# A routed expert layer on one core: the residual split of the second weight half moves from GpSimd to VectorE in the tail slots

## The chip, the cores and the metric

One core of one Trainium2 chip. The time is the device time of one execution in microseconds (us). Three runs of the kernel before gave 1162.65, 1166.04 and 1166.87 us; their median is 1166.04 us.

## The reference

A causal convolution of 7 taps with softmax weights (8 heads, 24 channels each) runs over 8 sequences of 2880 rows and 192 channels. Its 23040 rows go to 16 experts: the row's best of 4 groups, then the best of 4 experts in that group. Cut to what matters here:

```python
for g in range(G):
    mask_g = g_idx == g
    xg = x[mask_g]
    ... # e_idx, e_w from softmax(xg @ w_expert[g])
    for e in range(Eg):
        mask_e = e_idx == e
        h = np.maximum(xg[mask_e] @ w1[g, e], 0.0)   # 192 -> 1024
        ye = h @ w2[g, e]                            # 1024 -> 192
        out[tok_idx] = g_w[...] * e_w[...] * ye      # rows of that expert
```

All of it is float32, and the results have to be of float32 quality.

## The kernel before, in words

**Routing, then slots.** The convolution and the routing run unit by unit and write each row and its id to tables in memory. The expert layer works in slots. A big slot takes 256 rows of one expert (two tiles of 128), a small one 128 rows. For each slot GpSimd issues indirect DMAs that gather the rows (tile `xg`, line 648) and, at its end, others that scatter the results to `out` (line 750).

**Split operands.** Each float32 operand is split in two parts that TensorE takes: a high part, written by ScalarE, and the residual, written as a subtraction. A weight set has four splits in `split(k)`: k = 0 makes `ah` (ScalarE, line 613) and `al` (line 614) out of the first 128 rows of w1; k = 1 makes `bh` (ScalarE, line 621) and `bl` (line 622) out of the other 64 rows, which are loaded twice; k = 2 and 3 make the halves of `cw` (lines 628 and 629) out of w2. The dictionary `eng` says which engine makes a residual; without an entry it is VectorE. The loads land in six `raw` buffers, four for each set, so a split that ends sets a buffer free for a load of a later set, which SyncE's queue issues.

**A big slot** has four steps. In each, `hidden` does 20 matmuls (line 679), ScalarE makes `hh` (line 684) and VectorE `hl` (line 685); three steps later `back` does 16 matmuls (lines 697 and 701) into two banks `po`. `finish` scales both banks on ScalarE (line 748), adds two halves on VectorE (`ys`, line 749) and scatters. **A small slot** has two steps: `hidden_small` (line 714), a transposition (line 722), `hh` on ScalarE (line 725) and `hl` on VectorE (line 726), and `back_small` with four matmuls on `hh` (line 734) and four on `hl` (line 740).

**The plan.** The first 62 of 98 slots are big ones. Then come nine groups: a small tail slot, two big slots of one regular expert, and a big tail slot. Tail slots take the rows left over of an expert that a table names at run time. In a group there are thus three weight sets: small tail, regular, big tail.

**The order of the work.** The slot loop calls `split_one` at given steps, but in each engine's queue the instructions stand in the order in which the framework's planner lists them by its own estimates of cost, dependences and places in the text; what is ready early can be listed ahead of its slot. Once listed, an engine takes them strictly in that order. So an instruction that waits holds up all that stand behind it in its queue.

The place that matters is in `open_slot`, where a tail slot's weights are opened and its first argument pair, row offsets, is read at run time:

```python
if pi == "tail":
    W = weights(*tail_regs(lambda c: tab[0][0:1, e, c:c + 1], 2), {1: nc.gpsimd})
```

Of the kernel before, what the change touches and what calls it, by code (L numbers as in the profile page):

```python
# [35 lines left out]
def conv_moe_kernel(  # L36
# [10 lines left out]
    nc = tc.nc  # L47
# [9 lines left out]
    def pin(on, ins):  # L57

        return tc.keep_in_program_order(ins) if on and pinned[0] else ins
# [529 lines left out]
    def weights(r1, r2, eng=None):  # L589
        eng = eng or {}  # L590
        raw = [wraw.tile([P, F], F32, name="raw") for _ in range(4)]
        ra, rb = raw[0], raw[1]
        HF = NF // 2
        rc = [r[:, 0:HF * D].rearrange("p (f d) -> p f d", d=D) for r in raw[2:]]
        npin[0] += 1
        hold = tc.keep_in_program_order if NPIN[0] < npin[0] <= NPIN[1] else lambda ins: ins
        hold(nc.sync.dma_start(out=ra, in_=w1f[bass.ds(r1, P), :]))
        hold(nc.sync.dma_start(out=rb[0:D2], in_=w1f[bass.ds(r1 + P, D2), :]))
        hold(nc.sync.dma_start(out=rb[D2:P], in_=w1f[bass.ds(r1 + P, D2), :]))
        for k in range(2):  # L600
            hold(nc.sync.dma_start(
                out=rc[k], in_=w2f[bass.ds(r2 + k * HF * P, HF * P), :].rearrange("(f p) d -> p f d", p=P),
            ))
        W = {}

        def split(k):
            if k == 0:
                W["ah"] = ah = wsp.tile([P, F], F32R, name="ah")
                W["al"] = al = wsp.tile([P, F], F32R, name="al")
                if 8 in eng:  # L610
                    nc.gpsimd.tensor_copy(out=ah, in_=ra)
                else:
                    pin(PINA, nc.scalar.activation(out=ah, in_=ra, func=AF.Copy))  # L613
                eng.get(k, nc.vector).tensor_tensor(out=al, in0=ra, in1=ah.bitcast(F32), op=ALU.subtract)  # L614
            elif k == 1:
                W["bh"] = bh = wsp.tile([P, F], F32R, name="bh")
                W["bl"] = bl = wsp.tile([P, F], F32R, name="bl")
                if 9 in eng:
                    nc.gpsimd.tensor_copy(out=bh, in_=rb)
                else:  # L620
                    pin(PINB, nc.scalar.activation(out=bh, in_=rb, func=AF.Copy))  # L621
                eng.get(k, nc.vector).tensor_tensor(out=bl, in0=rb, in1=bh.bitcast(F32), op=ALU.subtract)
            else:
                if k == 2:
                    W["cw"] = wsp.tile([P, NF, 2, D], F32R, name="cw")
                cw = W["cw"]
                fs = slice((k - 2) * HF, (k - 1) * HF)
                pin(PINW, nc.scalar.activation(out=cw[:, fs, 0, :], in_=rc[k - 2], func=AF.Copy))  # L628
                eng.get(k, nc.vector).tensor_tensor(  # L629
                    out=cw[:, fs, 1, :], in0=rc[k - 2], in1=cw[:, fs, 0, :].bitcast(F32), op=ALU.subtract,  # L630
                )

        W["todo"] = [lambda k=k: split(k) for k in range(4)]
        return W
# [9 lines left out]
    def gather(ids, known, n=2):  # L644
        xs = xg[nslot[0] % NXG]
        nslot[0] += 1
        for t in range(n):
            nc.gpsimd.indirect_dma_start(  # L648
                out=xs[:, t, :], out_offset=None, in_=xcd[0:known, :],
                in_offset=bass.IndirectOffsetOnAxis(ap=ids[:, t:t + 1].bitcast(U32), axis=0),  # L650
                bounds_check=known - 1, oob_is_err=False,
            )
        return xs
# [251 lines left out]
    def stages_to(n):  # L905
        extra = sum(max(0, stages(n) - i * SKEW2) for i in range(1, LIVE2)) if n < NU else 0
        return sum(stages(u) for u in range(n)) + extra
# [7 lines left out]
    def step():  # L915

        if routed[0] < NU and len(live) < lead[1] and (not live or max(live, key=lambda a: a[0])[1] >= (lead[0] or SK[min(routed[0], len(SK)) - 1])):
            u = routed[0]
            live.append([u, 0, unit(u, xin0 if u == 0 else None)])
            routed[0] += 1  # L920
        if not live:
            return
        done[0] += 1
        cur = live.pop(0)
        cur[1] += 1
        try:
            next(cur[2])
            live.append(cur)
        except StopIteration:
            pass  # L930
# [17 lines left out]
    tab = [None]  # L948
# [19 lines left out]
    def open_portion(pi):  # L968
        need, spe = portions[pi]
        rows = spe * 2  # L970
        idp = const.tile([P, E, rows], I32, name=f"idp{pi}")
        if pi == 0:
            pin(PINI, IQ.dma_start(
                out=idp,
                in_=idtab[0:E * CAP].rearrange("(e r) c -> e r c", e=E)[:, 0:P * rows, :].rearrange(
                    "e (p r) c -> p e (r c)", r=rows),
            ))
        else:
            ci = const.tile([1, E], I32, name=f"ci{pi}")
            nc.vector.tensor_copy(out=ci, in_=cons[0:1])  # L980
            _, base = nc.values_load_multi_w_load_instructions(
                ci, engines=[ET.SP], min_val=0, max_val=DUMMY - P * rows, skip_runtime_bounds_check_because=OOB_WHY,
            )
            for e in range(E):
                nc.sync.dma_start(
                    out=idp[:, e],
                    in_=idtab[bass.ds(base[e], P * rows), :].rearrange("(p r) c -> p (r c)", r=rows),
                )
        idps[pi] = idp
        consume(spe * SLOT)  # L990
        if pi + 1 == len(portions):
            late.append(open_tail())

    def tail_regs(get, n):
        return [
            nc.values_load(
                get(c), engines=[ET.SP], min_val=0, max_val=mv, skip_runtime_bounds_check_because=OOB_WHY,
            )
            for c, mv in ((0, (E - 1) * D), (1, (E - 1) * F), (2, DUMMY))[:n]
        ]  # L1000
# [18 lines left out]
    def tiles(i):  # L1019

        return 1 if plan[i][0] == "tail" and plan[i][1] >= NBIG else 2

    def open_slot(i):
        if i >= len(plan):
            return
        pi, e, s = plan[i]
        if closing:
            wait[0] -= 1
            if wait[0] <= 0 or closing[0] == pi:
                open_portion(closing.pop())  # L1030
        while pi != "tail" and pi not in idps:
            step()
            if closing:
                open_portion(closing.pop())
        rate[0] = max(
            [(stages_to(portions[q][0]) - done[0]) / (max(starts[q] - MARGIN - i, 1) * 2 * NF)
             for q in starts if q not in idps] + [0.0])
        if late:
            next(late[0], None)
        if pi == "tail":  # L1040
            W = weights(*tail_regs(lambda c: tab[0][0:1, e, c:c + 1], 2), {1: nc.gpsimd})
            ids = idps["tail"][:, e]
            known = N
        else:
            W = pre.pop(e if pi == 0 else None, None) or weights(e * D, e * F, PENG(pi, e)) if s == 0 else opened[i - 1][0]
            ids = idps[pi][:, e, 2 * s:2 * s + 2]
            known = sum(n for _, n in units[:portions[pi][0]]) * BT
        opened[i] = (W, ids)
        gathered[i] = gather(ids, known, tiles(i))
# [3 lines left out]
    while routed[1] < portions[0][0]:  # L1053
# [3 lines left out]
        for i in [i for i, kk in enumerate(KPRE) if kk == k]:  # L1057
            e, q = divmod(i, 5)
            if q == 0 and e < 2:
                pre[e] = weights(e * D, e * F, {k: nc.gpsimd for k in PREG[e]})  # L1060
            elif e < 2 and 4 * e + q <= KN:
                split_one(pre[e])
        k += 1
    open_slot(0)
    open_slot(1)
    for e in range(2, 2 + PRE2):
        pre[e] = weights(e * D, e * F)
# [78 lines left out]
    for i, (pi, e, s) in enumerate(plan):  # L1146
# [3 lines left out]
        W, ids = opened[i]  # L1150
# [10 lines left out]
        for f2 in range(steps):  # L1161
# [25 lines left out]
            if f2 == 0:  # L1187
                open_slot(i + 2)
# [39 lines left out]
```

## Time and profile before

| what | before |
|---|---|
| median of three runs | 1166.04 us (1162.65 to 1166.87) |
| the profiled execution | 1165.88 us, of it span 1164.1 us |
| PE (TensorE matmul) busy in the span | 1111.3 us, 95% |
| PEld (TensorE weight load) | 1079.1 us, 93% |
| DVE (VectorE) | 802.9 us, 69% |
| ACT (ScalarE) | 690.9 us, 59% |
| POOL (GpSimd) | 495.4 us, 43% |
| mean granted TensorE clock | 0.985 |

A row of a timeline is: start in us from the span's start, length in us, engine, line, operation, tile written and tiles read, partitions x elements, count, and in brackets how long the engine sat idle just before and what ended that. A row of the waits is: who waited, for whom, us in total, times, longest. TensorE's matmuls overlap, so two of its rows can cover the same time. SP is SyncE; a q behind an engine's name is its sequencer.

### The profile page before, as it was taken

The page shows a single profiled execution, that of the slowest core. Times are in us where ns is not written, and L with a number is a line of the kernel's source. Part 1 is how long each engine was busy: PE and PEld are TensorE (multiplying, and loading weights), DVE is VectorE, ACT ScalarE, POOL GpSimd, SP SyncE. Part 2 cuts the span into 40 slices and gives each one's busy share as a digit, 9 for nine tenths or more (in the row PEclk, how much of TensorE's full clock was granted, in tenths as well). Part 3 has the DMA queues.
Part 4 walks back from the last instruction along what each step waited for, and adds up shares of the span by engine and source line. Part 5 has one row for each costly group of instructions (what it writes and reads, how often), then busy time and mean ns, then how long its engine had stood idle before and what let it go on. Part 6 is the DMA issues. An engine that isn't in the chain of part 4 may idle for free. (4 is left out here: it accounts for less than half of the span.)

```text
span 1164.1 us, 23639 instructions
## 1 busy us (share of the span) xinstructions
PE 1111.3 (95%) x8468; PEld 1079.1 (93%) x8468; DVE 802.9 (69%) x1667; ACT 690.9 (59%) x1326; POOL 495.4 (43%) x432
## 2 busy tenths in 40 slices
PE   6889899999999999999999999999999999999995
PEld 5768899999999999999999999999999999999995
DVE  3666987887877676575678666666766777767672
ACT  4535556657665565646655555555676666767662
POOL 1003423333435343434435444445455655646542
PEclk9978999999999999999999999999999999999999
DMA  8989879988994565536454656545666577676740
GB/s 181 236 201 223 187 183 225 215 227 222 233 249 132 139 176 131 138 104 158 121 151 88 170 93 175 149 123 142 175 164 195 165 200 208 172 188 172 194 114 21
DMA packets 194090, 196.17 MB, mean 169 GB/s; under 512 B 49443, under 2 KB 171181, under 8 KB 193966
## 3 DMA queue, kind: packets, MB, share of 16 engines
q1 hardware_dynamic: 127424, 140.43, 45.9%
q0 software_dynamic: 18528, 36.09, 12.2%
q10 hardware_dynamic: 48014, 18.10, 7.7%
q8 instruction: 67, 1.10, 0.4%
q14 instruction: 57, 0.47, 0.1%
HBM read 159.08 MB, written 36.85 MB: 168 GB/s over the span
## 5 line engine op out<-in xcount | busy, mean ns | idle before, releaser
L697 PE MATMUL po<-cw,hh 128*128 128x384 f32 x1424 | 443.4, 369 | 1.4 <-ACT ys L748 1.4
L679 PE MATMUL ph<-xa,ah 128*128 128x256 f32 x1424 | 389.9, 296 | 3.6 <-DVE hl L685 2.0
L701 PE MATMUL po<-cw,hl 128*128 128x192 f32 x1424 | 356.8, 251 | 0.0
L648 POOL DMA_INDIRECT xg<-xcd,idp x160 | 181.3, 1133 | 377.7 <-ACT ys L748 338.0
L685 DVE SCALAR_TENSOR_TENSOR hl<-ph,hh 128x512 fp32r<-128x512 f32 x356 | 242.8, 686 | 142.5 <-ACT hh L684 127.9
L684 ACT ACTIVATE hh<-ph 128x512 fp32r<-128x512 f32 x356 | 211.3, 596 | 214.6 <-PE ph L679 166.6
L679 PEld LDWEIGHTS ph<-xa,ah 128*128 128x128 f32 x1424 | 271.5, 191 | 6.7 <-DVE hl L685 2.8
L701 PEld LDWEIGHTS po<-cw,hl 128*128 128x128 f32 x1424 | 272.8, 192 | 1.9
L697 PEld LDWEIGHTS po<-cw,hh 128*128 128x128 f32 x1424 | 268.8, 189 | 4.6 <-ACT ys L748 2.3
L750 POOL DMA_INDIRECT out<-ys,idp x160 | 191.9, 1199 | 75.3 <-issue 48.9
L679 PE MATMUL ph<-xb,bh 128*128 128x256 f32 x712 | 201.9, 284 | 0.1
L679 PE MATMUL ph<-xb,bl 128*128 128x256 f32 x712 | 201.8, 284 | 0.0
L679 PE MATMUL ph<-xa,al 128*128 128x256 f32 x712 | 201.6, 283 | 0.0
L748 ACT ACTIVATE ys<-po,xg 128x384 f32<-128x384 f32 x187 | 105.7, 580 | 94.2 <-PE po L701 66.8
L749 DVE TENSOR_TENSOR ys<-ys 128x192 f32<-128x192 f32 x187 | 82.3, 447 | 90.9 <-ACT ys L748 84.7
L679 PEld LDWEIGHTS ph<-xa,al 128*128 128x128 f32 x712 | 136.9, 192 | 1.8
L679 PEld LDWEIGHTS ph<-xb,bl 128*128 128x128 f32 x712 | 136.7, 192 | 0.0
L679 PEld LDWEIGHTS ph<-xb,bh 128*128 128x128 f32 x712 | 135.9, 191 | 0.8 <-issue 0.5
L629 DVE TENSOR_TENSOR cw<-raw,cw 128x768 fp32r<-128x768 f32 x132 | 125.2, 951 | 11.4 <-ACT cw L628 5.3
L628 ACT ACTIVATE cw<-raw 128x768 fp32r<-128x768 f32 x132 | 110.7, 843 | 0.1
L614 DVE TENSOR_TENSOR al<-raw,ah 128x1024 fp32r<-128x1024 f32 x66 | 80.8, 1224 | 38.3 <-ACT ah L613 27.2
L613 ACT ACTIVATE ah<-raw 128x1024 fp32r<-128x1024 f32 x66 | 70.1, 1062 | 32.7 <-PE ph L679 13.8
(222 smaller groups left out, 1444.5 us busy)
## 6 DMA issues: line engine op xcount, KB each, us to landing
raw<-in_moe_w SPq DMA_DIRECT2D x132, 384.0 KB
raw<-in_moe_w SPq DMA_DIRECT2D x66, 512.0 KB
raw<-in_moe_w SPq DMA_DIRECT2D x132, 256.0 KB
xcd<-xc ACTq DMA_DIRECT2D x13, 742.5 KB
xin<-in_x SPq DMA_DIRECT2D x7, 1134.0 KB
xin<-in_x SPq DMA_DIRECT2D x6, 1039.5 KB
xcd<-xcb ACTq DMA_DIRECT2D x13, 360.0 KB
xg<-xcd,idp POOLq DMA_INDIRECT x160
```

The source lines that it names most:

```text
L614: eng.get(k, nc.vector).tensor_tensor(out=al, in0=ra, in1=ah.bitcast(F32), op=ALU.subtract)
L628: pin(PINW, nc.scalar.activation(out=cw[:, fs, 0, :], in_=rc[k - 2], func=AF.Copy))
L629: eng.get(k, nc.vector).tensor_tensor(out=cw[:, fs, 1, :], in0=rc[k - 2], in1=cw[:, fs, 0, :].bitcast(F32), op=ALU.subtract,)
L648: nc.gpsimd.indirect_dma_start(out=xs[:, t, :], out_offset=None, in_=xcd[0:known, :], in_offset=bass.IndirectOffsetOnAxis(ap=ids[:, t:t + ...
L679: nc.tensor.matmul(out=hp[:, j], lhsT=wgt[:, fs], rhs=xx, start=i == 0, stop=i == len(ops) - 1)
L684: nc.scalar.activation(out=hh, in_=hp, func=AF.Relu)
L685: nc.vector.scalar_tensor_tensor(out=hl, in0=hp, scalar=0.0, in1=hh.bitcast(F32), op0=ALU.max, op1=ALU.subtract,)
L697: nc.tensor.matmul(out=oo[t][:, 0:2 * D], lhsT=hh[:, j, ts], rhs=cw[:, f].rearrange("p a d -> p (a d)"), start=f == 0, stop=False,)
L701: nc.tensor.matmul(out=oo[t][:, 0:D], lhsT=hl[:, j, ts], rhs=cw[:, f, 0, :], start=False, stop=f == NF - 1,)
L748: nc.scalar.activation(out=ys[:, t, :], in_=oo[t][:, 0:2 * D], func=AF.Copy, scale=g)
L749: nc.vector.tensor_tensor(out=ys[:, t, 0:D], in0=ys[:, t, 0:D], in1=ys[:, t, D:2 * D], op=ALU.add)
L750: nc.gpsimd.indirect_dma_start(out=outviews[nscat[0] % len(outviews)], out_offset=bass.IndirectOffsetOnAxis(ap=ids[:, t:t + 1].bitcast(U32 ...
```

## The change

The tail slots' call loses its dictionary, so their 18 residuals `bl` are made by VectorE's `tensor_tensor` instead of GpSimd's. Operands, shapes and places in the text stay as they are. Nothing else is edited; the planner lists all queues anew.

```diff
         if pi == "tail":
-            W = weights(*tail_regs(lambda c: tab[0][0:1, e, c:c + 1], 2), {1: nc.gpsimd})
+            W = weights(*tail_regs(lambda c: tab[0][0:1, e, c:c + 1], 2))
             ids = idps["tail"][:, e]
```

The line in `split` that it decides:

```python
eng.get(k, nc.vector).tensor_tensor(out=bl, in0=rb, in1=bh.bitcast(F32), op=ALU.subtract)
```

## Rows read from the trace of the kernel before

**Rows 1.** Busy us of each engine in stretches, then granted clock, DMA share, GB/s.

```profile
450.00:790.00 340.00, 337.81 (x2643) 334.97 (x2643) 229.18 (x464) 193.27 (x358) 148.48 (x132) 1.00 0.54 134
821.60:1121.20 299.60, 292.31 (x2180) 284.75 (x2179) 212.56 (x319) 200.81 (x354) 164.53 (x130) 1.00 0.68 185
```

**Rows 2.** Waits of all engines, stretch 790 to 1164.

```profile
ACT bh L621 <- DMA raw<-in_moe_w: 14.8, 7, 2.7
...
PEld po L740 <- DVE hl L726: 10.0, 8, 1.6
...
PE po L740 <- DVE hl L726: 7.4, 7, 1.3
```

**Rows 3.** Timeline of PE at the small slots' second steps.

```profile
871.60 0.69 PE L740 MATMUL po<-cw,hl 128*128 128x192 f32 x4 [1.03 <-DVE hl L726]
...
943.97 0.69 PE L740 MATMUL po<-cw,hl 128*128 128x192 f32 x4 [0.71 <-DVE hl L726]
...
980.24 0.69 PE L740 MATMUL po<-cw,hl 128*128 128x192 f32 x4 [0.95 <-DVE hl L726]
...
1016.27 0.69 PE L740 MATMUL po<-cw,hl 128*128 128x192 f32 x4 [0.75 <-DVE hl L726]
...
1126.31 0.69 PE L740 MATMUL po<-cw,hl 128*128 128x192 f32 x4 [1.31 <-DVE hl L726]
...
1128.06 0.34 PE L697 MATMUL po<-cw,hh 128*128 128x384 f32 x1
```

**Rows 4.** Timeline of DVE around the last small slot.

```profile
1113.91 1.22 DVE L622 TENSOR_TENSOR bl<-raw,bh 128x1024 fp32r<-128x1024 f32 x1
1115.05 0.42 DVE L666 TENSOR_TENSOR xa<-pm,xa 128x256 fp32r<-128x256 f32 x1
...
1121.67 2.51 DVE L749 TENSOR_TENSOR ys<-ys 128x192 f32<-128x192 f32 x2 [3.28 <-ACT ys L748]
1124.11 0.95 DVE L629 TENSOR_TENSOR cw<-raw,cw 128x768 fp32r<-128x768 f32 x1
1124.98 0.68 DVE L685 SCALAR_TENSOR_TENSOR hl<-ph,hh 128x512 fp32r<-128x512 f32 x1
1125.58 0.68 DVE L726 TENSOR_TENSOR hl<-pm,hh 128x512 fp32r<-128x512 f32 x1
```

**Rows 5.** Line 749 over the span: duration ns min/median/max, first and last start.

```profile
L749 DVE TENSOR_TENSOR ys<-ys x187: 294/358/2201, 124.6 to 1154.6; 128x192 f32<-128x192 f32 x187
```

**Rows 6.** Groups by line, stretch 821 to 1130: count, busy us, mean ns, idle before.

```profile
L749 DVE TENSOR_TENSOR ys<-ys 128x192 f32<-128x192 f32 x59 | 37.2, 645 | 35.3 <-ACT ys L748 35.0 <-issue 0.2
```

**Rows 7.** Line 622 over the span, by engine: duration ns min/median/max, first and last start.

```profile
L622 DVE TENSOR_TENSOR bl<-raw,bh x48: 1154/1217/1227, 54.4 to 1113.9; 128x1024 fp32r<-128x1024 f32 x48
...
L622 POOL TENSOR_TENSOR bl<-raw,bh x18: 2384/2398/2407, 803.8 to 1121.3; 128x1024 fp32r<-128x1024 f32 x18
```

**Rows 8.** Timeline of POOL, the last group's two residuals.

```profile
1104.33 2.40 POOL L622 TENSOR_TENSOR bl<-raw,bh 128x1024 fp32r<-128x1024 f32 x1
...
1121.26 2.39 POOL L622 TENSOR_TENSOR bl<-raw,bh 128x1024 fp32r<-128x1024 f32 x1 [6.38 <-ACT bh L621]
```

**Rows 9.** Timeline of ACT around the last small slot.

```profile
1120.12 1.06 ACT L621 ACTIVATE bh<-raw 128x1024 fp32r<-128x1024 f32 x1 [2.61 <-SPq L1091]
1121.08 1.03 ACT L748 ACTIVATE ys<-po,xg 128x384 f32<-128x384 f32 x2
1122.01 0.84 ACT L628 ACTIVATE cw<-raw 128x768 fp32r<-128x768 f32 x1
1122.74 0.59 ACT L684 ACTIVATE hh<-ph 128x512 fp32r<-128x512 f32 x1
1123.22 0.60 ACT L725 ACTIVATE hh<-pm 128x512 fp32r<-128x512 f32 x1
...
1127.04 0.58 ACT L748 ACTIVATE ys<-po,xg 128x384 f32<-128x384 f32 x1 [1.02 <-PE po L740]
```

**Rows 10.** Timeline of DVE beside the small set's residual, last group.

```profile
1105.68 0.69 DVE L685 SCALAR_TENSOR_TENSOR hl<-ph,hh 128x512 fp32r<-128x512 f32 x1 [1.65 <-ACT hh L684]
1106.65 0.69 DVE L685 SCALAR_TENSOR_TENSOR hl<-ph,hh 128x512 fp32r<-128x512 f32 x1 [0.27 <-ACT hh L684]
```

## The prediction

> **What bounds the kernel now.** I read the busy shares first: TensorE is near full, so only what keeps it waiting can move the time. The stretches come next [rows 1]. In the 340 us of regular slots TensorE is busy 337.81 us, 2.2 us short; in the tail groups 292.31 of 299.60, 7.3 us short, at the full granted clock of 1.00 in both. VectorE is busy 212.56 of 299.60 there (71%), GpSimd 164.53 (55%). The waits of that part say who holds TensorE up: nearly all of it is one line, the four small-slot matmuls on `hl`, which wait for VectorE's line 726, 7.4 us in 7 cases; its weight loads wait 10.0 us in 8 cases for the same [rows 2]. The two views tell of the same gaps and differ because matmuls overlap, so the true loss lies between 7.4 and 10.0 us; I take the middle, 8.7. The PE timeline shows the cases: 1.03, 0.71, 0.95, 0.75 us, and 1.31 in each of the last three groups, of which one stands there [rows 3]. Nothing in that list names the GpSimd residual itself.
>
> **Why VectorE is late there.** In the last group it runs the pair of `ys` additions in 2.51 us, then a `cw` half, an `hl`, and at 1125.58 the `hl` that TensorE waits for [rows 4]. An addition of this shape has a median of 358 ns over the span, but a longest one of 2201 [rows 5]; the 59 of the tail have a mean of 645 [rows 6], which is 59 x (645 - 358) = 16.9 us too much, 1.88 us for each of nine groups. The first of the pair starts at 1121.67, while GpSimd works on its residual from 1121.26 to 1123.65 [rows 8], and VectorE goes on only after that: 2.51 us from 1121.67 end at 1124.18. So the residual on GpSimd, 2398 ns [rows 7], costs VectorE 2.51 - 2 x 0.36 = 1.79 us in the very stretch that TensorE waits on. This is the residual of the big tail slot's set, which the planner lists two slots ahead, in the small slot. The other nine (the small set's) lie beside `hl` instructions with an input in PSUM, which take their usual 0.69 us [rows 8, 10] and are not held up.
>
> **Removed.** 18 GpSimd instructions of 2398 ns, 43.2 us of an engine that is idle 45% of the stretch and for which TensorE is not seen to wait there: worth nothing by itself. With them goes GpSimd's wait for `bh`, 6.38 us ahead of the last one [rows 8], behind which gathers and scatters stood; these are issued earlier, and I count nothing for it. With them goes also the stall of 1.79 us in nine groups.
>
> **Added.** 18 VectorE instructions of 1217 ns [rows 7], 1.14 us from start to next start (1113.91 to 1115.05) [rows 4], together 20.5 us. Nothing in the trace shows them in their new places. The ends are 0, all in idle time, and +20.5 us, all on TensorE's path. For the nine of the small sets I take 0: `bl` would follow its `bh`, where GpSimd started at 1104.33, and VectorE sits idle 1.65 us before 1105.68 and 0.27 before 1106.65 [rows 8, 10], which is more than 1.14. With that cover gone it is 1.14 us late for one `hl`, 10.3 us in nine groups at most, and only where TensorE waits for that `hl`, which the waits do not show.
>
> For the nine of the big sets the place decides. When `bh` is done, VectorE has been idle for a while (3.28 us before the pair [rows 4]) and nothing else is ready, so I expect the planner to list `bl` there, ahead of the `ys` pair. It then starts about when GpSimd's did, 1121.26, and the rest follows: 1.14 for `bl`, 2 x 0.36 for the pair, 0.87 and 0.60 from start to start for `cw` and `hl` [rows 4]. Line 726 starts at 1121.26 + 1.14 + 0.72 + 0.87 + 0.60 = 1124.59, 0.99 us earlier than 1125.58. ScalarE's inputs are there in time: `ys` by 1122.11, `cw` by 1122.85, `hh` by 1123.33 and 1123.82 [rows 9]. The new wait, VectorE on `bh`, has the pair, `cw`, `hl` and line 726 behind it, and TensorE behind these; but their inputs stand behind `bh` in ScalarE's queue as well [rows 9], so they would wait anyway.
>
> **Buffers and queues.** `bl` is done earlier (1.22 us after `bh` instead of 2.40), so the `raw` buffer that it frees goes to SyncE's next load sooner, never later. ScalarE's `bh` waits for such a load 7 times, 14.8 us [rows 2]; I leave that as it is. No DMA is added.
>
> **Sum.** The waits of TensorE shrink by 0.99 each: 1.03 to 0.04, the three of 1.31 to 0.32, the others to nothing, so about 1.0 us stays. 8.7 - 1.0 = 7.7 us off. The profiled execution took 1165.88 us (span 1164.1, and 1.8 around it), which makes 1158.2; the median of the runs is 0.16 above it, so 1158.4. What is late next in those places is `hh` of line 725, done at 1123.82 [rows 9].
>
> [...] The additions are float32 with two inputs in SBUF, and the long one that is shown ends when GpSimd's residual does [rows 4, 8]. [...]
>
> **Rivals.**
> 1. *Half the gain.* `bl` is listed behind the `ys` pair instead of ahead of it. Then line 726 starts at 1121.67 + 0.72 + 1.14 + 0.87 + 0.60 = 1125.00, 0.58 earlier; 7 x 0.58 = 4.1 us by TensorE's waits, up to 4.8 at the scale of 8.7: 1161.6 us. For it: the pair comes from an older slot and may be preferred. Against it: idle time ahead of it.
> 2. *The wait moves.* The planner does not seem to know the stall (it listed the pair there), so in its reckoning line 726 comes later than before, and it may list the ten matmuls of the next `hidden` half (1.2 us) ahead of the four on `hl`. The small slot's bank is then emptied 1.2 us later, and the next `back` waits for it: today line 748 ends at 1127.62 and `back` starts at 1128.06, 0.44 us of room [rows 3, 9]. So 1.2 - 0.44 = 0.76 us, nine times, 6.8 of the 7.7 us are given back: 1165.3 us, no change.
> 3. *Slower: the stall isn't GpSimd's.* The long `ys` stays at 2.2 us for another reason, for instance its input. Then the pair starts 1121.26 + 1.14 - 1121.67 = 0.73 us later than now and all behind it too: 9 x 0.73 = 6.6 us more, 1172.6 us. It decides from the point where the longest line 749 is still near 2201 ns without GpSimd's residual. Against it: in the row pair GpSimd's end and VectorE's go together, and the excess comes to nine times the stall, as often as GpSimd makes such a residual there.
> 4. *More.* `bl` goes behind line 726, in a later gap; the whole wait of 7.4 to 10.0 us goes: 1156 to 1158.6. This counts to the forecast, since the time is nearly the same.
>
> **How the numbers follow.** Forecast with rival 4: 0.60, its own range 1156 to 1160.5. Rival 1: 0.18. Rival 2: 0.13. Rival 3, with any other loss on VectorE's longer queue: 0.09. Faster or slower begins at 0.5%, 5.8 us, about what a measurement of this kernel can tell from no change, so at 1160.2 and 1171.9. Faster: all of the forecast, 0.60. Same: rivals 1 and 2 and a little of rival 3, 0.32. Slower: 0.08. The range begins at the end of the unknown, 10.0 us off and a little for the spread of runs, 1155, and reaches over rivals 1 and 2 to 1167; rival 3 is left out.
>
> **What would show it.** In the changed trace line 749 has no instruction over 0.5 us; 66 residuals of line 622 stand on DVE; in the nine small slots `bl` stands right ahead of the `ys` pair; TensorE's waits for line 726 fall from 7.4 us to about 1; its busy share in the groups rises towards that of the regular slots. The prediction is wrong if those waits go and the time stays (rival 2: look for new waits of line 697 on line 748), or if the long `ys` stays.

## The result, and the profile after

The changed kernel took 1155.69 us (median of 4 runs, 1152.3 to 1159.08) beside 1166.45 us of the kernel before: a ratio of 0.9898, interval 0.9864 to 0.9932. It is faster, as forecast, but by 1.02% where 0.65% stood in the prediction, and 0.9898 lies just below the range's lower end (1155 / 1166.04 = 0.9905). The miss is narrow: the recorded ratio is not the quotient of the two medians, which would be 0.9908, just inside. Timed again, in 12 runs beside 35 of the kernel before, the ratio was 0.9927 (0.9902 to 0.9951), which is 8.5 us of 1161.78. The ratios, here and below, leave out a run more than 1.5% above the fastest of its kernel, one of those 35 and one of the kernel with one input from PSUM.

The profiled execution took 1159.08 us, of it span 1157.3 us. The first and last starts on TensorE of lines 714 and 740 bound the tail stretch, from the first small slot to the last matmul on `hl`; columns are count, ns min/median/max, first and last start in us.

```profile
L714 PE MATMUL ph<-ah,xa x36: 393/404/414, 824.5 to 1109.8; 128*128 128x512 f32 x36
...
L740 PE MATMUL po<-cw,hl x72: 250/274/358, 835.1 to 1119.9; 128*128 128x192 f32 x72
```

It lasts 1119.9 - 824.5 = 295.4 us. In the profile of before the same two starts are 821.7 and 1126.7, 305.0 us apart:

```profile
L714 PE MATMUL ph<-ah,xa x36: 393/404/414, 821.7 to 1115.0; 128*128 128x512 f32 x36
...
L740 PE MATMUL po<-cw,hl x72: 250/274/358, 832.3 to 1126.7; 128*128 128x192 f32 x72
```

So the tail is 9.6 us shorter. The head, in which both kernels have the same instructions in the same order but for the first moved residual, is 2.8 us longer, which is inside its spread between executions (816.2 to 824.5 us in the ten profiles). The busy us of the engines in stretches answer to [rows 1]:

```profile
450.00:790.00 340.00, 339.37 (x2669) 336.45 (x2669) 227.89 (x462) 192.78 (x355) 148.07 (x132) 1.00 0.54 135
824.50:1114.60 290.10, 289.81 (x2168) 283.05 (x2167) 216.05 (x335) 200.16 (x353) 130.47 (x114) 1.00 0.72 191
```

TensorE, the first number behind the length, is now 0.3 us short of full in the tail groups instead of 7.3, while VectorE (third) works more, 216.05 of 290.10 (74%). Both stretches are at the full granted clock (1.00). The waits that answer to [rows 2]:

```profile
DVE bl L622 <- ACT bh L621: 20.7, 8, 2.9
...
ACT bh L621 <- DMA raw<-in_moe_w: 16.8, 7, 2.7
...
PEld po L740 <- DVE hl L726: 1.9, 5, 0.4
```

The matmul row for line 726 (7.4 us in 7 cases) is gone and its weight loads' row fell from 10.0 to 1.9. The new wait is there, VectorE for `bh`, 20.7 us in 8 cases; no wait of TensorE for those instructions follows from it. VectorE, then ScalarE and TensorE around the last small slot, for [rows 4, 9, 3]:

```profile
1115.58 1.23 DVE L622 TENSOR_TENSOR bl<-raw,bh 128x1024 fp32r<-128x1024 f32 x1 [2.39 <-ACT bh L621]
1116.72 0.62 DVE L749 TENSOR_TENSOR ys<-ys 128x192 f32<-128x192 f32 x2
1117.26 0.95 DVE L629 TENSOR_TENSOR cw<-raw,cw 128x768 fp32r<-128x768 f32 x1
1118.13 0.68 DVE L685 SCALAR_TENSOR_TENSOR hl<-ph,hh 128x512 fp32r<-128x512 f32 x1
1118.73 0.68 DVE L726 TENSOR_TENSOR hl<-pm,hh 128x512 fp32r<-128x512 f32 x1
```

```profile
1114.49 1.06 ACT L621 ACTIVATE bh<-raw 128x1024 fp32r<-128x1024 f32 x1 [2.17 <-SPq L1091]
1115.46 1.03 ACT L748 ACTIVATE ys<-po,xg 128x384 f32<-128x384 f32 x2
...
1117.59 0.61 ACT L725 ACTIVATE hh<-pm 128x512 fp32r<-128x512 f32 x1
```

```profile
1118.86 0.86 PE L734 MATMUL po<-cw,hh 128*128 128x384 f32 x4
1119.56 0.60 PE L740 MATMUL po<-cw,hl 128*128 128x192 f32 x4
```

`bl` stands in VectorE's queue right ahead of the `ys` pair, and the pair takes 0.62 us instead of 2.51. From the start of `bh` to that of line 726 there are 4.24 us; before it was 1125.58 - 1120.12 = 5.46. So line 726 is 1.22 us earlier, and line 740 starts with no idle time ahead of it. Lines 749 and 622 over the span, for [rows 5, 7]:

```profile
L749 DVE TENSOR_TENSOR ys<-ys x187: 294/358/423, 125.1 to 1147.8; 128x192 f32<-128x192 f32 x187
```

```profile
L622 DVE TENSOR_TENSOR bl<-raw,bh x66: 1157/1216/1229, 52.9 to 1115.6; 128x1024 fp32r<-128x1024 f32 x66
```

No addition is over 0.5 us, and all 66 residuals are VectorE's. In the queues nothing else moved: TensorE (8468 matmuls), ScalarE (1326 instructions) and SyncE (435 transfers issued) have the same order of instructions in both kernels, VectorE has 18 more, and GpSimd 18 fewer, with its gathers and scatters in the same order.

### The profile page after: what moved, and what is told of

It is laid out like the page before. It is cut to its first block, busy times and chain, and to the rows that moved or that the text cites. A ratio compares the mean times of both kernels' runs of the same rounds, so it can differ in the third digit from the quotient of the medians.

```text
span 1157.3 us, 23621 instructions
## 1 busy us (share of the span) xinstructions
PE 1110.4 (96%) x8468; PEld 1079.6 (93%) x8468; DVE 806.5 (70%) x1685; ACT 691.5 (60%) x1326; POOL 457.2 (40%) x414
## 4 chain that ended last, share of the span: by engine, by line
PE 66%; issue 13%; DVE 7%; DMA 6%; POOL 5%; ACT 2%; POOLq 0%; another core or an unknown queue 0%; SPq 0%; ACTq 0%; DVEq 0%
PE ph L679 26%; PE po L697 16%; PE po L701 8%; PE pm L416 3%; POOL xg L648 3%; DMA raw<-in_moe_w 2%; POOL out L750 2%; PE pm L464 2%; DMA out<-ys,idpt 2%; PE pm L661 1%; PE pm L662 1%; PE pm L434 1%; PE pm L459 1%; DMA idtab<-lsi,rowi 1%; DVE hl L685 1%
## 5 line engine op out<-in xcount | busy, mean ns | idle before, releaser
L749 DVE TENSOR_TENSOR ys<-ys 128x192 f32<-128x192 f32 x187 | 65.4, 356 | 68.9 <-ACT ys L748 59.1
L622 DVE TENSOR_TENSOR bl<-raw,bh 128x1024 fp32r<-128x1024 f32 x66 | 80.3, 1217 | 22.3 <-ACT bh L621 22.0
```

## The experiments

The theory, called "port" (only a name: the runs show which instructions are held up, and for how long, not by what part of the chip): what costs is GpSimd reading SBUF while VectorE wants to read two inputs there, in the nine small slots. Rivals: GpSimd's queue (gathers and scatters held back by the residual's wait), VectorE's load, and something outside the tail. In all kernels below TensorE, ScalarE and SyncE have the order of before, so their traces can be laid side by side. GpSimd's gathers and scatters have it too, except in the kernel with one input from PSUM and the two in which GpSimd works beside VectorE, where some of them change places. The table gives the ratio to the kernel before with its interval, the tail stretch as above, TensorE's matmul waits for line 726, and the longest two-input `ys` addition.

| kernel | runs | ratio | tail, us | waits, us (times) | longest `ys`, ns |
|---|---|---|---|---|---|
| before | 4 | | 305.0 | 7.4 (7) | 2201 |
| before, again | 12 | 0.9999 (0.9974 to 1.0024) | 303.0 | 7.3 (8) | 2198 |
| after | 4 | 0.9898 (0.9864 to 0.9932) | 295.4 | 0 | 423 |
| after, again | 12 | 0.9927 (0.9902 to 0.9951) | 294.6 | 0 | 423 |
| big sets only | 12 | 0.9937 (0.9910 to 0.9964) | 294.3 | 0 | 424 |
| small sets only | 12 | 1.0041 (1.0017 to 1.0065) | 301.3 | 5.6 (7) | 2257 |
| small sets only, again | 12 | 1.0001 (0.9977 to 1.0024) | 303.9 | 8.2 (8) | 2252 |
| one input from PSUM | 12 | 0.9951 (0.9925 to 0.9976) | 294.4 | 0 | 2197 (once, in a slot ahead of the edit) |
| GpSimd reads beside | 6 | 1.0085 (1.0058 to 1.0113) | 309.7 | 10.5 (8) | 2062 |
| GpSimd writes beside | 12 | 0.9933 (0.9903 to 0.9962) | 295.1 | 0 | 425 |

**The changed kernel again**, no edit.

> The changed kernel unedited, timed in more rounds, since four runs leave the gain anywhere between 7.9 and 15.9 us. Theory 'port' (a GpSimd residual that reads SBUF holds up VectorE's ys addition in the nine small slots): the stretch from the first small slot to the last matmul on hl is again near 295.4 us (before: 305.1), and what is beyond 9.7 us in the timed gain is spread between runs, so the ratio settles near 0.992 (1156.5 us beside 1166). Rival 'more': something else in the kernel gained too; then the ratio stays at 0.990 or below and the head up to the first small slot is shorter than 821.7 us as well.

The tail is 294.6 us and the ratio 0.9927. It was not the changed kernel whose first four runs came out low (median 1155.69 us, and 1152.66 now) but the kernel before whose four came out high (1166.45 us, and 1161.78 now). The ratio is not 0.990 or below, and the head lasted 824.4 us here against 821.7 in the profile of before, so nothing points to a gain there; the rival falls.

**Big sets only.**

```diff
-            W = weights(*tail_regs(...), {1: nc.gpsimd})
+            W = weights(*tail_regs(...), {1: nc.gpsimd} if e >= NBIG else None)
```

> Only the nine big tail sets' residual bl goes to VectorE, the nine small sets' stay on GpSimd. Theory 'port': all of the gain, tail stretch 295.4 us, no ys addition over 0.5 us, time as the changed kernel (about 1156). Rival 'queue' (what gains is that GpSimd's queue no longer waits for bh, so gathers and scatters go out earlier): about half the gain, tail stretch near 300 us, time near 1161.

All of the gain with half of the change. The nine small sets' residuals stay on GpSimd, and that costs nothing.

**Small sets only**, the other half, and the same kernel once more.

```diff
-            W = weights(*tail_regs(...), {1: nc.gpsimd})
+            W = weights(*tail_regs(...), {1: nc.gpsimd} if e < NBIG else None)
```

> Only the nine small tail sets' residual bl goes to VectorE, the nine big sets' stay on GpSimd. Theory 'port': no gain, nine ys additions of 2.2 us stay, TensorE waits 7.4 us for line 726, tail stretch 305 us, time about 1166. Rival 'queue': half the gain, tail stretch near 300 us, time near 1161. Rival 'VectorE load' (each residual on VectorE costs TensorE something that the removed stall outweighed): slower than before, by up to 9 x 1.14 = 10 us.

> The small sets' nine residuals on VectorE once more, since 12 runs gave 0.41% slower [0.17, 0.65] where no change was expected, and its profile showed no longer wait. Theory 'port' with spread: the interval takes in 1.000 or misses it by less than 0.2%. Rival 'VectorE load': slower by 0.3 to 0.5% again, with a wait of TensorE for line 685 or for line 726 in the profile that the kernel before does not have.

No gain: the long additions and the waits stay. The first timing said 0.41% slower, the second 0.01%. TensorE's waits for line 726 are 5.6 and 8.2 us, on either side of the 7.4 and 7.3 of before, so I take the first timing as spread; a cost of VectorE's load isn't shown. VectorE and GpSimd in the last small slot of the second profile:

```profile
1115.03 2.58 DVE L749 TENSOR_TENSOR ys<-ys 128x192 f32<-128x192 f32 x2 [2.65 <-ACT ys L748]
...
1119.00 0.68 DVE L726 TENSOR_TENSOR hl<-pm,hh 128x512 fp32r<-128x512 f32 x1
```

```profile
1114.66 2.39 POOL L622 TENSOR_TENSOR bl<-raw,bh 128x1024 fp32r<-128x1024 f32 x1 [5.80 <-ACT bh L621]
```

The pair is held up to 1117.61 while GpSimd reads until 1117.05, as in [rows 4, 8]. That only the other half gains is what "port" says, but it doesn't yet rule out the queue: nearly all of GpSimd's wait for `bh` (53.0 us here, 53.1 in the kernel before) belongs to the big sets. The last pair of kernels does.

**One input from PSUM.** All residuals stay on GpSimd; in the tail the addition takes one half from the bank and scales it itself.

```diff
-            nc.vector.tensor_tensor(out=ys[:, t, 0:D], in0=ys[:, t, 0:D], in1=ys[:, t, D:2 * D], op=ALU.add)
+            nc.vector.scalar_tensor_tensor(out=ys[:, t, 0:D], in0=oo[t][:, D:2 * D], scalar=g,
+                in1=ys[:, t, 0:D], op0=ALU.mult, op1=ALU.add)   # from the tail on; as before ahead of it
```

> All 18 residuals stay on GpSimd as before; in the tail the ys addition reads one half straight from PSUM and scales it itself, so it has one input in SBUF instead of two. Theory 'port': GpSimd no longer holds it up, the additions take about 0.4 us, line 726 starts some 1.7 us earlier, TensorE's waits for it go, tail stretch near 296 us, time near 1157 without any residual moved. Rival 'queue' and any theory by which the residual itself must leave GpSimd: 1166, tail stretch 305 us, and a long addition stays.

The edit begins behind the pair of the first small slot, which keeps its long addition; in the other eight there is none, without moving any residual. The last small slot, VectorE and GpSimd:

```profile
1112.59 0.89 DVE L749 SCALAR_TENSOR_TENSOR ys<-po,xg,ys 128x192 f32<-128x192 f32 x2 [1.60 <-ACT ys L748]
1113.80 1.58 DVE L629 TENSOR_TENSOR cw<-raw,cw 128x768 fp32r<-128x768 f32 x1 [0.32 <-ACT cw L628]
1115.30 0.68 DVE L685 SCALAR_TENSOR_TENSOR hl<-ph,hh 128x512 fp32r<-128x512 f32 x1
1115.90 0.67 DVE L726 TENSOR_TENSOR hl<-pm,hh 128x512 fp32r<-128x512 f32 x1
```

```profile
1112.17 2.38 POOL L622 TENSOR_TENSOR bl<-raw,bh 128x1024 fp32r<-128x1024 f32 x1 [4.66 <-ACT bh L621]
```

The pair with one SBUF input runs inside GpSimd's time at its usual 0.42 us each. The next instruction with two, `cw`, starts at 1113.80 while GpSimd reads until 1114.55, and takes 1.58 us instead of 0.95: here it is the number of SBUF inputs that decides, not the line. Nor is it the operation: line 666, a `tensor_tensor` with one input in PSUM, starts beside the small sets' residuals eight times here and takes its usual 0.28 us.

The time is a different matter. TensorE's waits for line 726 are gone and the tail is 294.4 us, but only part of that comes from the addition. From the start of `bh` to that of line 726 there are 4.88 us instead of 5.47 (medians), so line 726 is 0.59 us earlier and not 1.7, because the stall has moved to `cw`. Reckoned as in the prediction, 0.59 us takes at most 7 x 0.59 = 4.1 us off the 7.4. The rest came in ahead of `bh`. ScalarE's wait for the load of `bh`, 14.8 us before, is short here:

```profile
ACT bh L621 <- DMA raw<-in_moe_w: 2.4, 3, 1.0
```

In every other kernel of the table it is between 13.1 and 16.8 us. GpSimd's gathers and scatters changed places around that load; whether this is why it lands earlier was not tested. So this kernel shows which instruction is held up, and it leaves open how much of its gain is owed to GpSimd's queue.

**GpSimd reads, or only writes, beside the pair.** Two kernels on top of the changed one. Behind `bl` of the big sets, GpSimd works on the raw buffer, which nobody reads any more.

```diff
+                if 99 in eng:  # a mark that the big tail sets carry; the first kernel
+                    nc.gpsimd.tensor_tensor(out=rb, in0=rb, in1=rb, op=ALU.subtract)
+                if 99 in eng:  # the second kernel
+                    nc.gpsimd.memset(rb, 0.0); nc.gpsimd.memset(rb, 0.0)
```

> The changed kernel, and in each of the nine big sets GpSimd does one more tensor_tensor of 128x1024 float32 on the raw buffer behind bl, in place, with a result that nobody reads: it reads SBUF and runs beside VectorE's ys pair and cw half. Theory 'port': a two-input instruction of VectorE that starts meanwhile (the second ys or the cw half) is held up until it ends, so nine instructions of over 2 us come back; line 726 then starts about 5.3 us after bh instead of the 4.3 of before, TensorE waits for it 9 x 2.4 = 22 us against 8.8, tail stretch near 315 us, time 8 to 12 us above the kernel before. Rival (the removed residual was only late work of its own, GpSimd holds nobody up): as the changed kernel, tail stretch 295 us.

> The same place and the same buffer, but GpSimd writes it twice with a memset (about 1 us each, by 0.43 us for 392 columns), so it reads nothing. Theory 'port, reads only' (what is shared is the way in which GpSimd reads SBUF and VectorE reads its second input): no long instruction on VectorE, tail stretch 295 us, time as the changed kernel. Rival 'port, any access' or 'any GpSimd work': VectorE is held up by about 2 us in nine places as beside the reading instruction, tail stretch over 305 us.

VectorE in the first, then in the second, with GpSimd of each behind it:

```profile
1127.00 1.23 DVE L622 TENSOR_TENSOR bl<-raw,bh 128x1024 fp32r<-128x1024 f32 x1 [2.21 <-ACT bh L621]
1128.14 2.33 DVE L749 TENSOR_TENSOR ys<-ys 128x192 f32<-128x192 f32 x2
...
1131.93 0.68 DVE L726 TENSOR_TENSOR hl<-pm,hh 128x512 fp32r<-128x512 f32 x1
```

```profile
1128.37 1.89 POOL L622 TENSOR_TENSOR raw<-raw 128x1024 f32<-128x1024 f32 x1 [7.07 <-DVE bl L622]
```

```profile
1110.90 1.23 DVE L622 TENSOR_TENSOR bl<-raw,bh 128x1024 fp32r<-128x1024 f32 x1 [2.47 <-ACT bh L621]
1112.04 0.62 DVE L749 TENSOR_TENSOR ys<-ys 128x192 f32<-128x192 f32 x2
1112.58 0.96 DVE L629 TENSOR_TENSOR cw<-raw,cw 128x768 fp32r<-128x768 f32 x1
```

```profile
1112.19 0.96 POOL L622 MEMSET raw<- 128x1024 f32 x1 [7.26 <-DVE bl L622]
```

A reading instruction brings the stall back (2.33 us for the pair) and the kernel is 0.85% slower than before; a writing one in the same place, beside the same pair, does nothing to VectorE, whose pair takes 0.62 us. (Of its two memsets one stands beside the pair, 0.96 us; the planner listed the other later. The two kernels have their gathers and scatters in the same order.)

The writing kernel also settles the rival "queue". GpSimd's queue waits there about as long as before (54.9 us for `bl`; before, 53.1 for `bh`), and the first gather behind that wait goes out 1114.72 - 1109.81 = 4.91 us after the start of `bh`, later than the 1123.80 - 1120.12 = 3.68 of before. GpSimd of before, then ScalarE, GpSimd and GpSimd's wait in the writing kernel:

```profile
1123.80 1.05 POOL L648 DMA_INDIRECT xg<-xcd,idpt  x1
```

```profile
1109.81 1.06 ACT L621 ACTIVATE bh<-raw 128x1024 fp32r<-128x1024 f32 x1 [2.26 <-SPq L1091]
```

```profile
1114.72 1.05 POOL L648 DMA_INDIRECT xg<-xcd,idpt  x1 [0.30 <-issue]
```

```profile
POOL raw L622 <- DVE bl L622: 54.9, 8, 7.7
```

The load of `bh` is waited for as in the other kernels (13.6 us), and the gain is that of the changed kernel, 0.9933. So the rival falls.

The size in the reading kernel was expected only in part: TensorE waits 10.5 us, not 22. The instruction is shorter than the residual (1.89 us instead of 2.40, with one tile as both inputs), so line 726 starts 6.02 us after the start of `bh`, 0.55 later than the 5.47 of before and not 1.0; and the 22 was summed wrongly, since 8.8 + 9 x 1.0 us makes 17.8. The tail grew by 309.7 - 304.0 = 5.7 us over the mean of the two profiles of before, near 9 x 0.55 = 5.0. The timed loss is 6.7 to 13.1 us; what makes up the rest stays open.

**The kernel before again**, no edit.

> The kernel before, unedited, timed against itself: the ratio tells what this measurement makes of no difference (0.2% either way is expected), and a second profile tells how much its tail stretch moves between executions. Theory 'port': nine ys additions near 2.2 us again, TensorE's waits for line 726 between 5 and 10 us. If the tail stretch comes out near 301 us instead of 305, the profile that the prediction was worked out from had longer waits than is usual.

The ratio is 0.9999, so the timing is fair to no difference. The tail is 303.0 us, between the two that were named: 2.0 us less than in the profile that the prediction used.

## Why the prediction was right or wrong

*What bounds the kernel.* Right. TensorE's waits for line 726 were all but the whole of its shortfall in the tail; with them gone it is 0.3 us short.

*Why VectorE is late.* Right, and shown from both sides: take the residual of the small slot away from GpSimd (big sets only), or one SBUF input from the addition, and the long addition goes; put another read there and it comes back. Rival 3 falls.

*The place of `bl`.* Right: ahead of the pair, in all nine groups, and TensorE's order did not change, so rivals 1 and 2 fall, and rival 4 with them.

*The nine small sets at 0.* Right. Their residual fell into VectorE's idle time; the `hl` behind it starts 0.23 us after its `hh` was done (1099.66), and the next one waits for ScalarE again:

```profile
1098.76 1.22 DVE L622 TENSOR_TENSOR bl<-raw,bh 128x1024 fp32r<-128x1024 f32 x1
1099.89 0.68 DVE L685 SCALAR_TENSOR_TENSOR hl<-ph,hh 128x512 fp32r<-128x512 f32 x1
1101.45 0.69 DVE L685 SCALAR_TENSOR_TENSOR hl<-ph,hh 128x512 fp32r<-128x512 f32 x1 [0.88 <-ACT hh L684]
```

Two kernels that differ in nothing else (after and big sets only) have ratios of 0.9927 and 0.9937.

*Buffers and queues.* Right: ScalarE waits for the load of `bh` 16.8 and 13.7 us in the two profiles of the changed kernel, 14.8 and 14.9 in those of before. That load is the next thing to look at in these groups, since the kernel with one input from PSUM, where it lands earlier, has no wait for line 726 left although its stall is only in part removed.

*The sum.* "8.7 - 1.0 = 7.7 us off" was a little short. Line 726 came 1.22 us earlier after `bh`, where 0.99 was worked out (I took 0.36 us for each addition; from start to start the pair takes 0.54 us), so of the 1.0 us that should stay TensorE's matmuls show nothing and its weight loads 1.9 us. The tail stretch fell from 305.0 and 303.0 to 295.4 and 294.6 us, 9.0 us by the means of two profiles each. Some 1.4 us of the first profile's tail were two gaps of 0.7 us on TensorE, at 836.69 and 912.57, that the second profile of before does not have, so I count them as a chance of that execution and no part of the change.

*The step that failed* is the size, at the lower end of the range; the mechanism held. The step reads: "The range begins at the end of the unknown, 10.0 us off and a little for the spread of runs, 1155". The end of the unknown was sound: the tail gave back 7.6 to 10.4 us in any pairing of the profiles. "A little", 1.0 us below 1156.0, was not. The kernel before ran between 1153.72 and 1172.91 us in its later runs, and the ten profiles have their first small slot between 816.2 and 824.5 us from the start, though TensorE's order of instructions is the same in all ten. Four runs of each kernel can differ by some us from that alone, and here they did: by the ratio 11.9 us where twelve runs gave 8.5, by the medians 10.8 and 9.1. Of the 4.2 us between 11.9 and the forecast's 7.7 the tail accounts for 1.3 (9.0 instead of 7.7, the sum above); the rest lies outside the stretch that the change touches, and with the twelve runs at 8.5 I put it down to spread. With the forecast at 0.9934 of the kernel before, the interval of the second measurement holds it.

What stays open is why the head varies by 8 us between executions of the same instructions. The traces show where it does: TensorE's 601st matmul already starts anywhere between 111.4 and 119.5 us in the ten profiles, and its 2101st between 309.7 and 317.8. From about 390 us to the first small slot the profiles keep their distances within 2 us.

## What to carry to other kernels

An instruction far longer than its median is a row to follow up even on an engine that is only 70% busy: look for what another engine does in exactly that time, since work moved to the busier engine can free it (here VectorE got 1.14 us more to do and was done 1.22 us earlier). Before a range is drawn for an effect under 1%, the spread of the runs at hand (here three runs over 4.2 us) has to go into it beside the unknowns of the sum.

## What the runs showed of the hardware

Here a float32 VectorE instruction with two inputs in SBUF that started while GpSimd read SBUF for a `tensor_tensor` was held until that ended, in every case: 2.19 us instead of 0.36 for an addition beside a residual (nine of nine before), 1.58 instead of 0.95 for a `cw` half (eight), and up to 2.06 for an addition beside the added read of the raw buffer. One with an input in PSUM ran at its usual time (0.69 us for `hl`, 0.42 for the scaled addition), and beside a GpSimd memset the two-input one did too (0.62 us for the pair).

A new wait cost nothing here, as the prediction had argued: VectorE stands 20.7 us in wait for `bh` with the pair, `cw`, `hl` and line 726 behind it, and TensorE's matmuls no longer wait for line 726 at all. The inputs of those instructions stand behind the same `bh` in ScalarE's queue.
